# Moving the value sum's rounding and remainder behind the next score chunk's sigmoid in an attention kernel with two matrix layers

## The chip, the cores and the metric

The kernel runs on one core of a Trainium2 chip. The metric is the device time of one launch in microseconds (us). The engines that matter here are PE (TensorE: PE rows are matmuls, PEld rows are its weight loads), ACT (ScalarE), DVE (VectorE) and SP, whose only work is to issue transfers (DMAs) between the chip's main memory and on-chip memory. Every engine works through its own queue of instructions strictly in order. PSUM is the on-chip memory that matmuls write into.

## The reference

Batch 4, 12 heads, 448 positions, head width 64; then two layers with 768 model columns and 2048 hidden columns over 1792 tokens.

```
scores = scale * np.matmul(q, k.transpose(0, 1, 3, 2)) - np.log(S)
attn = 1.0 / (1.0 + np.exp(-scores))                 # sigmoid attention: no row sums
x = np.matmul(attn, v)                               # (B, H, S, D) -> (B * S, H * D)
h = x @ w_in1;  g = h - np.tanh(h);                  y = g @ w_out1
h = y @ w_in2;  r = np.maximum(h, 0.0);  g = s * (r * r) + b;  out = g @ w_out2
```

## The kernel before, in words

The work goes through the chip in two passes, each over two of the four batches: attention for twelve units, then layer 1, then layer 2. A **unit** is one batch and one pair of heads; units are numbered 0 to 23 over both passes, so that pass 1 has units 0 to 11 and pass 2 has units 12 to 23. The weights arrive as 8-byte words in pass 1; they are converted to float32 there (`w_conv`) and split into a rounded part and a remainder (`w_split`), and a float32 copy is written out for pass 2. The first three conversions and two splits lie between the attention units 5 to 9.

Most matmul operands are kept as a pair: a rounded upper part, made on ACT as a copy with a cast, and the remainder, made on DVE as the difference. The function `split` does that for the value sum.

The functions for one unit, all in program order on every engine (`keep_in_program_order`, line 80):

- `prep(i)` transposes q and k of unit i on PE into a PSUM tile `tqk`, lets ACT cast `qt` and `kt` from it, lets DVE make their remainders, and last lets DVE copy a piece to `qkf`, after which the tile is free.
- `qk(i, c)` makes the scores of one chunk of keys and applies the sigmoid on ACT (`af<-sc`). Chunk 3 has eight small matmuls from `qkf`; the chunks 0, 1 and 2 have six matmuls each from `qt` and `kt` and a sigmoid over 128x896.
- `av(i)` multiplies the sigmoid's tiles with the values (PSUM tiles `o` and `o2`). It is a generator: up to its `yield` stand the twenty matmuls of the trace; behind it ACT copies `o2` to `half`, DVE adds `half` to `o`, ACT casts `o` to `x` (the upper part), and DVE makes the remainder of `x`.

The main loop (lines 490 to 506) works on several units at once. One turn i issues the scores of chunks 0 and 1 of unit i, the conversion or split that is due, `prep(i + 1)`, the matmuls of `av(i - 1)`, chunk 3 of unit i, the rest of `av(i - 1)`, the loads of unit i + 3, and chunk 2 of unit i:

```
a = av(i - 1) if i > i0 else iter(())
next(a, None)
qk(i, 3)
now(a)
qkv_load(i + 3)
qk(i, 2)
```

On PE the scores of chunk 2 of unit i, and of chunks 0 and 1 of unit i + 1, stand directly behind each other, eighteen matmuls in all, and the transposes of unit i + 2 follow. The tiles `sc` and `tqk` share three PSUM buffers of two banks each (`banks`, tag "two"): a new tile has to wait until the reader of the tile that was in its buffer before is done. The transposes of `prep(i + 2)` go into the buffer that chunk 2 of unit i used. The tiles `o` and `o2` share two buffers of one bank each (tag "one").

q, k and v of a unit come in nine transfers of SP (`qkv_load`).

Of the kernel before, what the change touches and what calls it, by code (L numbers as in the profile page):

```python
# [19 lines left out]
def tile_kernel(ctx, tc, q, k, v, w_in1, w_out1, w_in2, w_out2, s_in, b_in, out):  # L20
# [63 lines left out]
    def banks(name):  # L84
        return ps_p.tile([P, 2, 512], F32, tag="two", name=name, bufs=3)
# [77 lines left out]
    def upto(step, n):  # L163

        while done[step] <= n:
            yield from step(done[step]) or ()
            done[step] += 1
# [10 lines left out]
    def now(g):  # L178
        for _ in g:
            pass  # L180
# [7 lines left out]
    def split(hi, lo, t):  # L188
        act.copy(hi, t)
        dve.tensor_tensor(out=lo, in0=t, in1=hi.bitcast(F32), op=ALU.subtract)  # L190
# [4 lines left out]
    def qkv_load(i, what="qkv"):  # L195
        if i >= B * NP:
            return
        b, hs = i // NP, slice(i % NP * 2, i % NP * 2 + 2)
        if "q" in what:
            raws[i] = {"r": at_p.tile([P, 2, D], F32, tag="rawr", name="rawr", bufs=3)}  # L200
        for nm in what:
            src = {"q": q, "k": k, "v": v}[nm]

            dma = act if i == 0 and nm == "k" else sp
            rest = src[b, hs, SM:S, :].rearrange("h p d -> p h d")
            if nm == "v":
                t = at_p.tile([P, 2, NJ + 1, D], F32, tag="rawv", name="rawv", bufs=4)

                tt, last = t[:, :, 0:NJ, :], t[0:RM, :, NJ, :]
                dma.dma_start(out=t[RM:P, :, NJ, :], in_=rest)  # L210
                dma.dma_start(out=tt.rearrange("p e j d -> p e (j d)"), in_=src[b, hs, 0:SM, :].rearrange("h (p j) d -> p h (j d)", p=P))
            else:
                t = at_p.tile([P, NJ, 2, D], F32, tag=f"raw{nm}", name=f"raw{nm}", bufs=3)

                o = RM * ((nm == "k") ^ (b % 2))
                last = raws[i]["r"][o:o + RM]
                for e in range(2):
                    dma.dma_start(out=t[:, :, e, :], in_=src[b, hs.start + e, 0:SM, :].rearrange("(p j) d -> p j d", p=P))
            dma.dma_start(out=last, in_=rest)
            raws[i][nm] = t  # L220

    def prep(i):

        if i >= B * NP:
            return
        b = i // NP
        rq, rk, rr = (raws[i][nm] for nm in "qkr")
        both = banks("tqk") if i else None


        if i:
            flat = both.rearrange("p a b -> p (a b)")
            parts = [(flat, 0), (flat, SM + P), (flat, SM)]
        else:

            one = [ps_p.tile([P, 512], F32, tag="one", name="tqk0", bufs=2) for _ in range(2)]
            parts = [(one[0], 0), (one[1], P), (one[0], SM), (one[1], 0)]
        for (ps, o), r in zip(parts, (rk, rq) if b % 2 else (rq, rk)):
            for j in range(NJ):
                pe.transpose(ps[:, o + j * P:o + (j + 1) * P], r[:, j].rearrange("p h d -> p (h d)"), ident)  # L240
        for ps, o in parts[2:]:
            pe.transpose(ps[:, o:o + P], rr.rearrange("p h d -> p (h d)"), ident)
        tq, tk = (flat[:, 0:S], flat[:, S:2 * S]) if i else (one[0][:, 0:S], one[1][:, RM:P + SM])
        if b % 2:
            tq, tk = tk, tq
        qt = at_p.tile([P, 2, S], F32R, tag="qt", name="qt", bufs=2)
        kt = at_p.tile([P, 2, S], F32R, tag="kt", name="kt", bufs=2)
        act.copy(qt[:, 0], tq)
        act.copy(kt[:, 0], tk)
        for t, ps in ((qt, tq), (kt, tk)):  # L250
            dve.tensor_tensor(out=t[:, 1], in0=ps, in1=t[:, 0].bitcast(F32), op=ALU.subtract)

        flt[i] = tmp_p.tile([P, WN], F32, tag="t2", name="qkf", bufs=2)
        dve.tensor_copy(flt[i], (flat if i else one[0])[:, SM:S + S] if b % 2 else (flat if i else one[0])[:, 0:S + RM])
        ready[i] = qt, kt
        avs[i] = []

    def qk(i, c):

        b = i // NP  # L260
        qt, kt = ready[i]
        sc = banks("sc")
        if c == NJ:

            f = flt.pop(i)
            kl, qf = (f[:, 0:RM], f[:, RM:]) if b % 2 else (f[:, S:], f[:, 0:S])
            for h in range(2):
                for e in range(2):
                    hs = slice(e * D, e * D + D)
                    pe.matmul(sc[h * RM:h * RM + RM, e, :SH], kl[hs], qf[hs, h * SH:h * SH + SH], start=True, stop=True)  # L270
            avs[i].append(g_p.tile([P, 2, 2, S], F32, tag="g", name="af", bufs=4))
            act.activation(avs[i][-1][:, 1, :, :SH], sc[:, :, :SH], AF.Sigmoid, bias=nlogs, scale=SCALE)
            return
        k0 = c * P if b % 2 else c * P + RM
        for n, (wi, xi) in enumerate(((0, 0), (0, 1), (1, 0))):
            for e in range(2):
                hs = slice(e * D, e * D + D)
                pe.matmul(sc[:, e, :S], kt[hs, wi, k0:k0 + P], qt[hs, xi], start=n == 0, stop=n == 2)
        if c == 0:
            avs[i].append(g_p.tile([P, 2, 2, S], F32, tag="g", name="af", bufs=4))  # L280
        act.activation(avs[i][-1][:, c % 2], sc[:, :, :S], AF.Sigmoid, bias=nlogs, scale=SCALE)

    def av(i):

        b, hp = i // NP, i % NP
        rv, af = raws.pop(i)["v"], avs.pop(i)
        o = ps_p.tile([P, 512], F32, tag="one", name="o", bufs=2)[:, :S]

        o2 = ps_p.tile([P, 512], F32, tag="one", name="o2", bufs=2)[:, :SH]
        for c in range(NJ):  # L290
            for e in range(2):
                pe.matmul(o[e * D:e * D + D], rv[:, e, c, :], af[c // 2][:, c % 2, e], start=c == 0, stop=False)
        for h in range(2):
            for e in range(2):
                ks = slice(h * RM, h * RM + RM)
                pe.matmul((o2 if h else o[:, :SH])[e * D:e * D + D], rv[ks, e, NJ, :], af[1][ks, 1, e, :SH], start=h == 1, stop=True)
        yield
        half = tmp_p.tile([P, WN], F32, tag="t1", name="half", bufs=2)[:, :SH]
        act.copy(half, o2)
        dve.tensor_tensor(out=o[:, SH:], in0=o[:, SH:], in1=half, op=ALU.add)  # L300
        if b % 2 == 0:
            x_t[b // 2, hp] = x_p.tile([P, 2, T2], F32R, tag="x", name="x1", bufs=CC)
        ns = slice(b % 2 * S, b % 2 * S + S)
        xt = x_t[b // 2, hp]
        split(xt[:, 0, ns], xt[:, 1, ns], o)
# [182 lines left out]
    for sb in range(B // 2):  # L488
        i0, i1 = sb * 2 * NP, (sb + 1) * 2 * NP
        for i in range(i0, i1):  # L490
            if i == 0 or i > i0:
                qk(i, 0)
                qk(i, 1)

            for at, step, n in ((2, w_load, 1), (4, w_load, 2), (5, w_conv, 0), (6, w_split, 0), (7, w_load, 3), (7, w_conv, 1), (8, w_split, 1), (9, w_load, 4), (9, w_conv, 2)):
                if i == at:
                    now(upto(step, n))
            if i + 1 < i1:
                prep(i + 1)
            a = av(i - 1) if i > i0 else iter(())  # L500
            next(a, None)
            qk(i, 3)
            now(a)
            qkv_load(i + 3)
            qk(i, 2)
            ready.pop(i)
        order = [(0, range(CC - 2)), lambda: now(av(i1 - 1)), (1, range(CC - 1)), (0, range(CC - 2, CC)), (1, [CC - 1])]

        turn[0] = 3
        x2 = layer1(sb, order)  # L510
        last = sb + 1 == B // 2
        order = [(0, range(CC - 1)), (1, range(CC - 1)), (0, [CC - 1]), (1, [CC - 1])]
        layer2(sb, x2, order, {} if last else {2: lambda: prep(i1), 4: lambda: qk(i1, 0), 6: lambda: qk(i1, 1)})
# [30 lines left out]
```

## Time and profile before

| | |
|---|---|
| median of three runs | 1125.86 us (1124.82 to 1127.56) |
| the profiled execution | 1124.64 us, of which the span is 1122.8 us |
| PE busy | 1098.6 us, 98% of the span |
| DVE, ACT busy | 585.5 us (52%), 493.7 us (44%) |
| granted TensorE clock | 1.0 |

The profiled execution is 1.22 us below the median of the runs and 1.84 us longer than its own span. The profile gives for each engine its instructions in order of time, how long the engine stood idle ahead of one and which event ended that wait. A share of busy time is a mean over the attention parts and the layers, which differ.

### The profile page before, as it was taken

The numbers are of one execution on the slowest core, as the hardware profiler recorded it, in microseconds if no ns is written. First come the engines' busy times: TensorE is split into PE (matmuls) and PEld (weight loads), VectorE is DVE, ScalarE is ACT, GpSimd is POOL, SyncE is SP. The second block draws the span as 40 slices with busy tenths as digits, with TensorE's granted clock in tenths as the row PEclk, the third lists the DMA queues.
The fourth block names the chain that finished last, engine by engine and source line by source line (L and its number), as shares of the span: only waits on it lengthen the run. The fifth ranks groups of instructions, "written<-read, shape, count | busy, mean of one in ns | idle before, by whom it ended". The sixth has DMA issues, their size and how long they took to land.

```text
span 1122.8 us, 15139 instructions
## 1 busy us (share of the span) xinstructions
PE 1098.6 (98%) x6077; PEld 949.4 (85%) x6077; DVE 585.5 (52%) x878; ACT 493.7 (44%) x782; POOL 0.7 (0%) x6
## 2 busy tenths in 40 slices
PE   8899999999999999999998899999999999999998
PEld 4446889888889999898964578898888899999998
DVE  3453656767787668686633332343434541434343
ACT  5775444242446563635356643332313363515060
POOL 0000000000000000000000000000000000000000
PEclk9999999999999999999999999999999999999999
DMA  4765454546455645454444301121211121211102
GB/s 112 201 152 148 156 185 154 169 146 192 127 169 168 203 136 183 133 189 130 167 113 113 79 29 57 48 66 43 71 43 46 54 71 43 60 53 57 57 15 99
DMA packets 115430, 124.47 MB, mean 111 GB/s; under 512 B 56480, under 2 KB 90784, under 8 KB 115360
## 3 DMA queue, kind: packets, MB, share of 16 engines
q1 hardware_dynamic: 114416, 123.27, 36.6%
q8 instruction: 48, 0.79, 0.3%
q10 hardware_dynamic: 944, 0.23, 0.1%
q14 instruction: 22, 0.18, 0.0%
HBM read 92.80 MB, written 30.67 MB: 110 GB/s over the span
## 4 chain that ended last, share of the span: by engine, by line
PE 92%; DMA 3%; DVE 2%; ACT 2%; SPq 1%; issue 1%; ACTq 0%; DVEq 0%
PE h L80 42%; PE z L80 21%; PE y L80 20%; PE o L80 6%; PE sc L80 2%; PE tqk L80 2%; SPq L80 1%; ACT af L80 1%; DMA rawq<-in_q_dram 1%; DMA rawv<-in_v_dram 1%; DMA rawk<-in_k_dram 1%; DMA win<-wf 1%; DVE wa L80 0%; DVE o L80 0%; DVE qt L80 0%
## 5 line engine op out<-in xcount | busy, mean ns | idle before, releaser
L80 PE MATMUL h<-x,whi 128*128 128x512 f32 (+1 forms) x1536 | 434.4, 363 | 0.0
L80 PEld LDWEIGHTS h<-x,whi 128*128 128x128 f32 x1536 | 283.4, 188 | 33.9 <-issue 1.3
L80 PE MATMUL h<-x,wlo 128*128 128x512 f32 (+1 forms) x768 | 279.8, 364 | 0.0
L80 PE MATMUL z<-whi,g 128*128 128x384 f32 x896 | 229.5, 334 | 0.0
L80 PE MATMUL y<-g,whi 128*128 128x512 f32 (+1 forms) x768 | 218.6, 366 | 0.2 <-DVE y L80 0.2
L80 ACT ACTIVATE t<-h 128x512 f32<-128x512 f32 (+1 forms) x128 | 69.6, 544 | 234.3 <-PE h L80 233.7
L80 PEld LDWEIGHTS z<-whi,g 128*128 128x128 f32 x896 | 162.0, 188 | 0.6 <-issue 0.6
L80 PEld LDWEIGHTS y<-g,whi 128*128 128x128 f32 x768 | 142.4, 188 | 17.7 <-DVE y L80 0.6
L80 PEld LDWEIGHTS h<-x,wlo 128*128 128x128 f32 x768 | 144.1, 188 | 15.2
L80 DVE TENSOR_TENSOR wlo<-wf,whi 128x768 fp32r<-128x768 f32 x128 | 122.0, 953 | 59.7 <-ACT whi L80 59.7
L80 ACT CAST whi<-wf 128x768 fp32r<-128x768 f32 x128 | 106.1, 833 | 101.9 <-DVE wf L80 58.0
L80 PE MATMUL z<-wlo,g 128*128 128x384 f32 x448 | 149.7, 334 | 0.0
L80 PE MATMUL y<-g,wlo 128*128 128x512 f32 (+1 forms) x384 | 140.9, 367 | 0.0
L80 DVE TENSOR_TENSOR g<-t,g 128x512 fp32r<-128x512 f32 (+1 forms) x128 | 79.9, 624 | 83.5 <-ACT g L80 83.5
L80 ACT ACTIVATE af<-sc,nlogs 128x896 f32<-128x896 f32 (+1 forms) x96 | 83.1, 919 | 48.4 <-PE sc L80 39.0
L80 ACT CAST g<-t 128x512 fp32r<-128x512 f32 (+1 forms) x128 | 72.7, 568 | 33.2 <-DVE t L80 30.9
L80 DVE TENSOR_TENSOR t<-h,t 128x512 f32<-128x512 f32 x64 | 39.9, 623 | 85.4 <-ACT t L80 85.4
L80 PEld LDWEIGHTS z<-wlo,g 128*128 128x128 f32 x448 | 84.1, 188 | 0.0
L80 PEld LDWEIGHTS y<-g,wlo 128*128 128x128 f32 x384 | 72.1, 188 | 8.9 <-DVE wlo L80 0.4
L80 DVE TENSOR_TENSOR z<-z 128x384 f32<-128x384 f32 x84 | 45.2, 554 | 65.8 <-PE z L80 65.8
L80 PE MATMUL o<-af,rawv 128*64 128x448 f32 (+1 forms) x480 | 72.4, 478 | 0.0
L80 DVE TENSOR_TENSOR y<-y 128x512 f32<-128x512 f32 x72 | 41.5, 618 | 58.0 <-PE y L80 58.0
(42 smaller groups left out, 674.9 us busy)
## 6 DMA issues: line engine op xcount, KB each, us to landing
raw<-in_moe_w_in_dram SPq DMA_DIRECT2D x32, 768.0 KB, 5.2
raw<-in_moe_w_out_dram SPq DMA_DIRECT2D x32, 768.0 KB, 4.8
win<-wf SPq DMA_DIRECT2D x32, 384.0 KB, 2.6
wout<-wf SPq DMA_DIRECT2D x32, 384.0 KB, 2.6
wf<-win SPq DMA_DIRECT2D x32, 384.0 KB, 3.0
wf<-wout SPq DMA_DIRECT2D x32, 384.0 KB, 3.0
rawq<-in_q_dram SPq DMA_DIRECT2D x48, 96.0 KB, 2.7
rawv<-in_v_dram SPq DMA_DIRECT2D x24, 192.0 KB, 2.7
```

The source lines that it names most:

```text
L80: return lambda *a, **kw: tc.keep_in_program_order(getattr(self.engine, name)(*a, **kw))
```

## The change

`av` gets a second `yield`, between DVE's sum with `half` and the split of `o` into `x`. The main loop takes the first part of what stood behind the old `yield` (the copy to `half` and the sum) where it stood, and runs the rest (the cast to `x` and its remainder) behind chunk 2 of the scores.

```
         half = tmp_p.tile([P, WN], F32, tag="t1", name="half", bufs=2)[:, :SH]
         act.copy(half, o2)
         dve.tensor_tensor(out=o[:, SH:], in0=o[:, SH:], in1=half, op=ALU.add)
+        yield
         if b % 2 == 0:
             x_t[b // 2, hp] = x_p.tile([P, 2, T2], F32R, tag="x", name="x1", bufs=CC)
...
             a = av(i - 1) if i > i0 else iter(())
             next(a, None)
             qk(i, 3)
-            now(a)
+            next(a, None)
             qkv_load(i + 3)
             qk(i, 2)
+            now(a)
             ready.pop(i)
```

On ACT this is the queue of turn 1 of pass 1, before (-) and now (+). `af<-sc` with 128x2x224 is the sigmoid of chunk 3; the three with 128x896 are the sigmoids of chunk 2 of this unit and chunks 0 and 1 of the next; `x_270` and `x_291` are the same tile under two names.

```order
 L80 ACTIVATE af<-sc,nlogs 128x2x224
 L80 COPY half<-o_249 128x224
-L80 CAST x_270<-o 128x448
-L80 ACTIVATE af<-sc,nlogs 128x896 x3
+L80 ACTIVATE af<-sc,nlogs 128x896
+L80 CAST x_291<-o 128x448
+L80 ACTIVATE af<-sc,nlogs 128x896 x2
 L80 CAST qt<-tqk 128x448
 L80 CAST kt<-tqk 128x448
```

The cast to `x` and the sigmoid of chunk 2 have changed places; nothing else on ACT has moved. The same stands in turns 1 to 11 and 13 to 23.

On DVE the queue of that turn is the same as before but for the numbers in the names; the rows are those of the changed kernel. `o<-o,half` is the sum, the row of `x_291` is the remainder of the cast.

```order
L80 TENSOR_TENSOR o<-o,half 128x224
L80 TENSOR_TENSOR x_291<-o,x_291 128x448
L80 TENSOR_TENSOR qt<-tqk,qt 128x448
L80 TENSOR_TENSOR kt<-tqk,kt 128x448
L80 COPY qkf<-tqk 128x512
```

The remainder still stands ahead of the next unit's `qt`, `kt` and `qkf`, though it now waits for a cast that stands one sigmoid later on ACT.

At the end of pass 1, in turn 11, ACT has no further sigmoids behind the cast; `o_1123` belongs to the last value sum, which stands within layer 1.

```order
 L80 ACTIVATE af<-sc,nlogs 128x2x224
 L80 COPY half<-o_1064 128x224
-L80 CAST x_601<-o 128x448
-L80 ACTIVATE af<-sc,nlogs 128x896
+L80 ACTIVATE af<-sc,nlogs 128x896
+L80 CAST x_622<-o 128x448
 L80 COPY half<-o_1123 128x224
```

Here too the two have changed places. The queues of PE and SP hold the same instructions in the same order as before.

## Rows read from the trace of the kernel before

**Rows 1.** Windows: span A:B, length, busy of each engine, granted clock, DMA share, GB/s

```profile
14.00:95.00 81.00, 71.48 (x576) 38.45 (x574) 36.91 (x63) 56.55 (x89) 0.00 (x0) 1.00 0.66 166
142.00:300.00 158.00, 158.00 (x779) 141.04 (x778) 111.12 (x157) 62.86 (x97) 0.00 (x0) 1.00 0.54 168
575.00:649.00 74.00, 65.67 (x555) 37.11 (x553) 27.77 (x50) 49.65 (x81) 0.00 (x0) 1.00 0.39 95
```

**Rows 2.** PE's waits, 14 to 95 us (pass 1): total, times, longest

```profile
PE tqk L80 <- ACT af L80: 6.0, 7, 0.9
PE tqk L80 <- DMA rawq<-in_q_dram: 1.7, 2, 1.2
PE tqk L80 <- DMA rawk<-in_k_dram: 1.1, 2, 0.7
```

**Rows 3.** PE's waits, 560 to 650 us (pass 2)

```profile
PE tqk L80 <- ACT af L80: 4.6, 5, 0.9
PE tqk L80 <- DMA rawv<-in_v_dram: 3.7, 4, 0.9
```

**Rows 4.** Timeline of one turn of pass 2: start, busy, engine, instruction [idle before]

```profile
594.43 2.81 ACT L80 ACTIVATE af<-sc,nlogs 128x896 f32<-128x896 f32 x3
...
595.50 0.55 PE L80 MATMUL tqk<-ident,rawq 128*128 128x128 f32 x3 [0.91 <-ACT af L80]
...
597.11 0.55 ACT L80 CAST qt<-tqk 128x448 fp32r<-128x448 f32 x1
...
597.52 0.57 ACT L80 CAST kt<-tqk 128x448 fp32r<-128x448 f32 x1
...
598.82 0.21 PEld L80 LDWEIGHTS o<-af,rawv 64*64 64x64 f32 x8 [0.70 <-issue]
...
599.20 0.68 DVE L80 COPY qkf<-tqk 128x512 f32<-128x512 f32 x1
...
599.74 2.09 PE L80 MATMUL sc<-qt,kt 64*128 64x448 f32 x18
599.93 0.64 ACT L80 ACTIVATE af<-sc,nlogs 128x448 f32<-128x448 f32 x1 [1.84 <-PE sc L80]
...
600.47 0.34 ACT L80 COPY half<-o 128x224 f32<-128x224 f32 x1
600.84 0.40 DVE L80 TENSOR_TENSOR o<-o,half 128x224 f32<-128x224 f32 x1 [0.95 <-ACT half L80]
601.27 0.53 ACT L80 CAST x<-o 128x448 fp32r<-128x448 f32 x1 [0.47 <-DVE o L80]
601.70 2.81 ACT L80 ACTIVATE af<-sc,nlogs 128x896 f32<-128x896 f32 x3
601.84 0.62 DVE L80 TENSOR_TENSOR x<-o,x 128x448 fp32r<-128x448 f32 x1 [0.60 <-ACT x L80]
...
602.76 0.55 PE L80 MATMUL tqk<-ident,rawk 128*128 128x128 f32 x3 [0.94 <-ACT af L80]
```

**Rows 5.** Timeline of turn 9 in pass 1, which converts a weight chunk

```profile
77.17 0.55 PE L80 MATMUL tqk<-ident,rawk 128*128 128x128 f32 x3 [0.52 <-DMA rawq<-in_q_dram]
...
81.40 2.89 PE L80 MATMUL sc<-qt,kt 64*128 64x448 f32 x18
...
82.68 0.68 DVE L80 COPY qkf<-tqk 128x512 f32<-128x512 f32 x1
...
85.19 0.55 PE L80 MATMUL tqk<-ident,rawk 128*128 128x128 f32 x3 [0.91 <-ACT af L80]
```

**Rows 6.** The chain that ended last, pass 1: start, length, what

```profile
35.23 4.29 DMA rawk<-in_k_dram
39.66 0.63 PE tqk L80 x4
```

**Rows 7.** k's transfers of unit 10: issue times, time from issue to landing

```profile
L80 SPq DMA_DIRECT2D rawk<-in_k_dram x2: 604/612/619, 70.3 to 71.0; - x2
...
DMA to landing us min/median/max: 4.2/4.4/4.6
```

**Rows 8.** SP's own waits, 14 to 100 us, the largest total

```profile
SPq L80 <- PE sc L80: 1.1, 3, 0.7
```

More of the change, by code (lines that the diff above doesn't have):

```diff
@@ L300, in av @@
         dve.tensor_tensor(out=o[:, SH:], in0=o[:, SH:], in1=half, op=ALU.add)
+        yield
         if b % 2 == 0:
@@ L502, in tile_kernel @@
             qk(i, 3)
-            now(a)
+            next(a, None)
             qkv_load(i + 3)
             qk(i, 2)
+            now(a)
             ready.pop(i)
```

## The prediction

> **What bounds the kernel now.** I read the windows first. In the layers PE has no idle time: 158.00 us busy of 158.00 [rows 1]. What the change does can therefore only be earned in the two attention stretches, where PE is busy 71.48 of 81.00 us and 65.67 of 74.00 us [rows 1]; and since PE is the bound right behind each stretch, what is earned there should stay earned to the end. Next I read what PE waits for. In pass 2 it is one gap, nine times, 4.6 + 3.7 = 8.3 us, always ahead of the transposes `tqk` [rows 3]. In pass 1 the same gap stands with 6.0 us in 7 waits, and beside it 1.7 + 1.1 us in 4 waits for q and k [rows 2].
>
> The timeline of one turn shows where the gap comes from [rows 4]. Let t be the start of the eighteen score matmuls, 599.74. ACT runs the sigmoid of chunk 3 at t + 0.19, the copy `half` at t + 0.73, then stands idle 0.47 us until DVE has made the sum, casts `x` at t + 1.53, and only at t + 1.96 starts the sigmoid of chunk 2, whose six matmuls are the first of the eighteen and long over. The transposes need the PSUM buffer that this sigmoid reads; they start 1.06 us after it, at t + 3.02, though the eighteen end at t + 2.09. That is the 0.94 us of the gap. One turn lasts 602.76 - 595.50 = 7.26 us.
>
> The four waits put down to `rawv` are the same gap: they have the same longest length, 0.9 [rows 3], and the transposes read q and k, not v. I count them as waits for the sigmoid.
>
> **The change, part by part.** It adds no instruction and no transfer. It takes the sum's round trip through DVE and the cast out of the way of chunk 2's sigmoid, and puts the cast, and with it the remainder, one sigmoid later.
>
> *The sigmoid of chunk 2.* It can start when `half` is off ACT and its six matmuls are done. A cast of 0.53 us lets the next instruction start 0.43 us after it (601.27 to 601.70), so `half` with 0.34 us should take about 0.24, which gives t + 0.97. Six of eighteen matmuls take a third of 2.09, t + 0.70, and somewhat more until the last one's result is there. I take t + 1.00. The transposes follow 1.06 us later, at t + 2.06, or when the eighteen are over, at t + 2.09. So they move from t + 3.02 to t + 2.09, which is 0.93 us per turn [rows 4]. Below, the gain could be nothing, if something else holds the transposes; above, it cannot exceed the gap, 0.94.
>
> *The next bound.* With a turn of 7.26 - 0.93 = 6.33 us, another ring has to be looked at: ACT and DVE must have freed the next unit's `tqk` buffer when chunk 0 wants it [rows 4]. From t: sigmoid of chunk 2 at + 1.00; the pitch of a large sigmoid is (597.11 - 594.43) / 3 = 0.89; so the cast starts at + 1.89, the two other sigmoids at + 2.32 and + 3.21, the cast `qt` at + 4.10, `kt` 0.41 later at + 4.51, `qkf` 599.20 - 597.52 = 1.68 after that at + 6.19, over at + 6.87. Chunk 0 wants the buffer about 0.70 into the next eighteen, and a wait takes 0.04 us to end where `x`'s remainder waits for its cast (601.80 to 601.84), which I round up to at most 0.2. So the next t cannot come before + 6.21 to + 6.37. It is as tight as PE's own path. I take 6.35 us for the turn, a gain of 0.91.
>
> *The remainder and what is queued behind it.* `x`'s cast moves from t + 1.53 to t + 1.89 and its remainder from 601.84 to about 602.2, over at 602.8. Behind it on DVE wait `qt`, `kt` and `qkf`, which need casts that come later still, at + 4.10; so it holds up nothing. PE waits for it as well, since `o2` of the next value sum takes the buffer it reads; that part of the value sum starts 598.82 - 595.50 = 3.32 us after the transposes, by the new times at about t + 5.4, against t + 3.1. In the turn that ends a pass the cast is some 0.4 us late, and `x` is first wanted in layer 1, several us behind. Cost nothing; cover 2 us or more.
>
> *Pass 2.* Nine gaps [rows 3], 0.91 each: 8.2 us. Ends: 0 and 8.3.
>
> *Pass 1* is different, because transfers stand beside the gap. SP issues without pause: its largest total of waits over 86 us is 1.1 us [rows 8]. So the q and k of a unit land when SP and the DMA engines get to them, and not earlier because PE is ahead. Two landings bind. k of unit 5 lands at 35.23 + 4.29 = 39.52, and its transposes start at 39.66 [rows 6]: everything gained up to there is lost again, as PE waits for this today. From there the gaps are regained, each about 0.9, some more in turns where a weight chunk is converted, until unit 10. The second of its two k transfers is issued at 71.0 and lands 4.6 later, at 75.6 [rows 7], where the transposes now start at 77.17 [rows 5]. Without the landing they would come 3 us earlier or more (four of the seven waits for the sigmoid, 0.86 each on the mean [rows 2], lie between 39.66 and these transposes); with it, 77.17 - 75.6 = 1.57 us. Turn 9, from there to 85.19, is 8.02 us long: it has a gap of 0.91, and its eighteen matmuls take 2.89 instead of 2.09, as chunk 1 waits there for `qkf`, over at 83.36, behind a weight conversion [rows 5]. The conversion doesn't wait for these transposes, so it runs ahead by what was gained before the landing, and `qkf` should be done by about 80.5, before chunk 1 wants it at 81.3. Of the 0.80 I leave 0.2 to be waited for (chunk 3's sigmoid ends at t + 0.83 [rows 4] and frees a buffer here too). That is 0.91 + 0.6 = 1.5. Pass 1: 1.57 + 1.5 = 3.1 us. Ends: 0, if SP sets the pace to the end, and 6.0 + 1.7 + 1.1 = 8.8, if no landing binds.
>
> What the row on SP shows, a queue that hardly waits [rows 8], has a rule in the Trainium skill, Perfetto Trace Analysis, section What "DMA-bound" means: a stretch is DMA-bound where the issuing engine's track is solid with transfers. By that rule alone pass 1 would give nothing and the sum would be 8.2; by the landings against PE's waits, 2.8 us for transfers and 6.0 for the sigmoid [rows 2], it gives 3.1.
>
> *Sum.* 8.2 + 3.1 = 11.3 us. The profiled execution took 1124.64, so 1113.3; it stood 1.22 below the median of the runs, 1125.86, which gives 1114.6. I say 1114.
>
> **The rivals.**
>
> *Pass 1 is held by its transfers to the end.* If k of unit 11 or q of unit 10 lands later than I read, or a faster PE meets the landings of every unit, only pass 2 gains: 8.2 us, 1116.4 to 1117.7. For it speaks that SP never rests; against it, that 7 of the 11 waits in pass 1 are for the sigmoid.
>
> *No landing binds in pass 1.* The rows of one execution give single landings; the two that bind took 4.29 and up to 4.6 us [rows 6, 7]. Were such ones 2 us quicker, pass 1 would give 6 to 8.8 and the time would be 1107 to 1111. Against it: the landing at 39.52 is on the chain that ended last [rows 6].
>
> *The gap stays and only changes its cause.* It is a wait for a PSUM buffer, and no buffer is added. If the ring through ACT and DVE, which I put at 6.35 us, is really 0.9 longer, because a few waits take 0.2 more than I read, chunk 0 waits for `qkf` in place of the transposes waiting for the sigmoid, and the turn stays at 7.26: 1124 to 1127. Against it: every link of the ring but one, the pitch of `half`, stands in a row. The Trainium skill, Perfetto Trace Analysis, section Optimization Strategy, says of a gap that repeats that it can mean too little SBUF or PSUM for the next tile; by that rule this change, which adds no buffer, leaves the gap. The trace agrees that a buffer is waited for, but shows its reader sitting ready on ACT for about 1 us, held by order alone.
>
> *Slower: the sigmoid becomes a cork.* Today the cast goes while chunk 2's matmuls run; now it, the remainder on DVE and all that is queued behind both wait until those matmuls are done. If PE reached chunk 2 late, the whole ring would slip by as much. From 0.91 us of delay beyond t + 1.00 it eats the gain, and each 0.3 us more costs 0.3 in some 20 turns, 6 us: 1131. Against it: on PE the six matmuls stand at the head of the eighteen, at t itself, and nothing in the rows holds them there.
>
> **How the numbers follow.** My forecast gets 0.63, the held pass 1 0.16, the free pass 1 0.08, the unchanged gap 0.08, the cork 0.05. Faster by more than 0.3% (3.4 us, about what a measurement of this kernel can tell from no change) holds in the first three: 0.87; same 0.08; slower 0.05. The range reaches from 1109, most of the way into the free pass 1, to 1119, which takes in the held pass 1 and a pass 2 that gives 0.2 us less per turn; outside are some 2 in 10.
>
> **What would show it.** In the changed profile the sigmoid of chunk 2 starts about 1.0 us after the eighteen and directly behind `half`; ACT's 0.47 us of idle time ahead of the cast is gone. PE's waits ahead of `tqk` in pass 2 fall from 8.3 us to under 1, and the turn from 7.26 to about 6.35, perhaps with small waits of chunk 0 for `qkf`. In pass 1 the waits for the sigmoid shrink while those for q and k grow, above all at units 5 and 10, the first at the same 39.66. Layer 1 starts about 3 us earlier in pass 1, about 11 in pass 2, and the layers' lengths stay. I would be wrong if the transposes in pass 2 still waited 0.5 us or more, or if PE waited in the layers for weights that now come too late.

## The result, and the profile after

The changed kernel takes 1115.53 us (median of 4 runs, 1113.83 to 1117.16), the kernel before in the same comparison 1125.34 (4 runs, 1124.77 to 1127.56). The ratio is 0.9909, with a 95% interval from 0.9888 to 0.993. The profiled execution took 1114.92 us, with a span of 1113.1; before it was 1124.64 and 1122.8, so the two executions differ by 9.7 us, where the sum of the prediction says 11.3.

The first matmul of layer 1 (`h<-x,whi`) marks the end of an attention stretch, so its two starts split the gain between the passes. In the timeline of PE before they read:

```profile
95.58 0.74 PE L80 MATMUL h<-x,whi 128*128 128x512 f32 x2
...
649.46 0.74 PE L80 MATMUL h<-x,whi 128*128 128x512 f32 x2
```

and after:

```profile
94.26 0.74 PE L80 MATMUL h<-x,whi 128*128 128x512 f32 x2
...
639.76 0.73 PE L80 MATMUL h<-x,whi 128*128 128x512 f32 x2
```

Up to the first mark 95.58 - 94.26 = 1.32 us are gained. Between the marks it is 649.46 - 95.58 = 553.88 against 639.76 - 94.26 = 545.50, which is 8.38 us. Together that is 9.70, the whole difference of the spans; the layers behind the second mark neither gain nor lose.

**Pass 2.** PE's waits from 565 to 645 us after the change are one row (engine, line, tile, releaser: total, times, longest), where [rows 3] has nine gaps with 8.3 us:

```profile
PE sc L80 <- ACT af L80: 0.3, 1, 0.3
```

One turn of pass 2 after, from its eighteen score matmuls to the next (start, busy, engine, instruction, idle before), beside [rows 4]:

```profile
589.30 2.17 PE L80 MATMUL sc<-qt,kt 64*128 64x448 f32 x18
589.49 0.63 ACT L80 ACTIVATE af<-sc,nlogs 128x448 f32<-128x448 f32 x1 [1.46 <-PE sc L80]
...
590.02 0.34 ACT L80 COPY half<-o 128x224 f32<-128x224 f32 x1
590.25 1.02 ACT L80 ACTIVATE af<-sc,nlogs 128x896 f32<-128x896 f32 x1
590.39 0.40 DVE L80 TENSOR_TENSOR o<-o,half 128x224 f32<-128x224 f32 x1 [0.57 <-ACT half L80]
591.15 0.54 ACT L80 CAST x<-o 128x448 fp32r<-128x448 f32 x1
...
591.40 0.55 PE L80 MATMUL tqk<-ident,rawq 128*128 128x128 f32 x3
...
591.73 0.62 DVE L80 TENSOR_TENSOR x<-o,x 128x448 fp32r<-128x448 f32 x1 [0.93 <-ACT x L80]
...
593.35 0.57 ACT L80 CAST qt<-tqk 128x448 fp32r<-128x448 f32 x1
...
595.46 0.68 DVE L80 COPY qkf<-tqk 128x512 f32<-128x512 f32 x1
...
595.63 0.67 PE L80 MATMUL sc<-qt,kt 64*128 64x448 f32 x4
```

With t = 589.30, chunk 2's sigmoid starts at t + 0.95, directly behind `half`; the cast follows at t + 1.85 with no idle time; the transposes start at t + 2.10, without a wait, as the eighteen end. The next eighteen come 595.63 - 589.30 = 6.33 us later. From the transposes at 578.75 to those at 629.31, eight turns later, a turn is 6.32 us on the mean, against 7.26 before.

**Pass 1.** PE's waits from 14 to 93 us, where [rows 2] has 6.0 us for the sigmoid and 2.8 for q and k:

```profile
PE tqk L80 <- DMA rawk<-in_k_dram: 3.7, 4, 1.5
PE tqk L80 <- DMA rawq<-in_q_dram: 0.6, 1, 0.6
PE sc L80 <- ACT half L80: 0.4, 2, 0.2
PE tqk L80 <- ACT x L80: 0.3, 1, 0.3
```

The waits for the sigmoid are gone here as well, but those for q and k have grown from 2.8 to 4.3 us. They have really grown by 2.0: of the 2.8 us, the 0.52 ahead of unit 10's transposes at 77.17 [rows 5] belong to the sigmoid, since that unit's q had landed at 74.12 and its k at 75.59. The chain that ended last (start, length, what) shows where the k of units 5 and 10 landed:

```profile
35.87 5.23 DMA rawk<-in_k_dram
...
41.23 0.63 PE tqk L80 x4
...
72.09 4.90 DMA rawk<-in_k_dram
76.98 0.14 issue
77.12 0.95 PE tqk L80 x7
```

In [rows 6] the first landing was at 39.52 and the transposes at 39.66; here they are at 41.23, later than before. In [rows 5] unit 10's transposes stood at 77.17, and here they stand at 77.12: all that was gained up to there is lost again.

Something else shows here that the kernel before had not shown. These are the windows of after (span A:B, length, busy of each engine, granted clock, DMA share, GB/s):

```profile
14.00:25.00 11.00, 8.52 (x67) 4.78 (x66) 3.13 (x6) 7.00 (x10) 0.00 (x0) 1.00 0.40 91
25.00:30.00 5.00, 5.00 (x31) 1.78 (x29) 1.75 (x3) 0.97 (x2) 0.00 (x0) 0.67 0.56 130
30.00:41.00 11.00, 9.14 (x82) 5.58 (x74) 3.80 (x7) 8.87 (x14) 0.00 (x0) 1.00 0.84 234
41.00:47.00 6.00, 5.77 (x34) 2.30 (x36) 1.75 (x3) 0.97 (x2) 0.00 (x0) 0.72 0.46 105
47.00:92.00 45.00, 43.99 (x346) 23.69 (x346) 26.05 (x43) 37.10 (x59) 0.00 (x0) 1.00 0.72 181
```

The granted TensorE clock has a mean of 0.67 and 0.72 in two of them, so it was at the lower of its two levels, 1.2 instead of 2.4 GHz, for a part of each. Both stretches begin with the end of a wait for k, in PE's timeline:

```profile
24.62 0.63 PE L80 MATMUL tqk<-ident,rawk 128*128 128x128 f32 x3 [1.47 <-DMA rawk<-in_k_dram]
...
25.40 4.44 PE L80 MATMUL o<-af,rawv 128*64 128x448 f32 x20
...
41.23 0.52 PE L80 MATMUL tqk<-ident,rawk 128*128 128x128 f32 x3 [1.45 <-DMA rawk<-in_k_dram]
```

The value sum behind the first wait takes 4.44 us; at the full clock it takes 3.02 (592.31 in the same trace).

### The profile page after: what moved, and what is told of

Read it like the earlier page. It is cut to its first block, busy times and chain, and to the rows that moved or that the text cites. A ratio compares the mean times of both kernels' runs of the same rounds, so it can differ in the third digit from the quotient of the medians.

```text
span 1113.1 us, 15139 instructions
## 1 busy us (share of the span) xinstructions
PE 1100.2 (99%) x6077; PEld 948.9 (85%) x6077; DVE 585.5 (53%) x878; ACT 491.9 (44%) x782; POOL 0.7 (0%) x6
## 2 busy tenths in 40 slices
DMA packets 115430, 124.47 MB, mean 112 GB/s; under 512 B 56480, under 2 KB 90784, under 8 KB 115360
## 4 chain that ended last, share of the span: by engine, by line
PE 94%; SPq 2%; DVE 1%; DMA 1%; ACT 1%; issue 0%; DVEq 0%; ACTq 0%
PE h L80 42%; PE z L80 21%; PE y L80 20%; PE o L80 6%; PE sc L80 4%; SPq L80 2%; PE tqk L80 1%; DMA rawk<-in_k_dram 1%; ACT af L80 0%; DVE wa L80 0%; DVE x L80 0%; DVE wf L80 0%; DVE y L80 0%; DVE wlo L80 0%; ACT x L80 0%
## 5 line engine op out<-in xcount | busy, mean ns | idle before, releaser
L80 ACT ACTIVATE af<-sc,nlogs 128x896 f32<-128x896 f32 (+1 forms) x96 | 86.1, 928 | 48.5 <-PE sc L80 39.1
L80 PE MATMUL o<-af,rawv 128*64 128x448 f32 (+1 forms) x480 | 75.5, 493 | 0.0
```

The source lines that it names most:

```text
L80: return lambda *a, **kw: tc.keep_in_program_order(getattr(self.engine, name)(*a, **kw))
```

## The experiments

The theory is that of the prediction: in pass 2 the order on ACT alone held PE; in pass 1 the gain is limited by when q and k land, and SP, which issues them, sets that. Its rivals: pass 1 gives nothing whatever the order; what matters is the place of the copy and the sum, not of the cast; what is lost in pass 1 is lost to something other than SP. The first four kernels ran on one chip against 1125.08 (15 runs of the kernel before), the next four against 1125.53 (7), the last two against 1124.74 (11). Each edit is against the changed kernel.

**pass2_only** has the new order in pass 2 alone.

```
-            next(a, None)
+            if sb == 1:
+                next(a, None)
+            else:
+                now(a)
             qkv_load(i + 3)
```

> The new order in pass 2 alone. Theory (in pass 2 the gap was pure order, in pass 1 the landing of unit 10's k takes most of it back): 8.3 us less than before, 1117, PE's waits ahead of the transposes in pass 2 near 0, pass 1 as before. Rival (both passes gain alike, the profiled execution of the changed kernel was unlucky in pass 1): also 8.3, so this run alone fixes the share of pass 2; what is left to the changed kernel's 9.8 is pass 1.

Measured: 1117.44 us, ratio 0.9926 (0.9913 to 0.9938). From the first `h` at 97.02 to that of pass 2 at 642.52 it is 545.50 us, as in the changed kernel: pass 2 gives 8.38 by itself. Pass 1, in the old order, ended 1.44 us later here than in the profile before. Its waits ahead of `tqk` are 8.9 us in all, as before (8.8 [rows 2]); but one value sum, at 25.59, took 4.52 us in place of 3.02, at a mean clock of 0.72 from 25 to 31 us. So pass 1 varies between executions of the same instructions.

**pass1_only** has it in pass 1 alone: the same edit with `sb == 0`.

> The new order in pass 1 alone. Theory (transfers hold pass 1): 1 to 2 us less than before, about 1124, with waits for k ahead of the transposes of units 3, 5 and 10 in place of those for the sigmoid. Rival (my sum): 3.1 us less, 1122.

Measured: 1122.77 us (11 runs, 1121.61 to 1126.03), ratio 0.998 (0.9971 to 0.9989): 2.3 us, between the theory's 1 to 2 and the rival's 3.1. The profiled execution, 1121.61 us, is the quickest of the 11, and it shows the prediction's own picture; four rows of PE's timeline:

```profile
38.33 0.52 PE L80 MATMUL tqk<-ident,rawq 128*128 128x128 f32 x3 [1.97 <-DMA rawq<-in_q_dram]
39.16 0.52 PE L80 MATMUL tqk<-ident,rawk 128*128 128x128 f32 x3 [0.30 <-DMA rawk<-in_k_dram]
...
75.62 0.52 PE L80 MATMUL tqk<-ident,rawk 128*128 128x128 f32 x3 [1.79 <-DMA rawk<-in_k_dram]
...
92.51 0.74 PE L80 MATMUL h<-x,whi 128*128 128x512 f32 x2
```

Unit 10 starts at 75.62, where 75.6 was forecast, and `h` at 92.51, 3.07 us ahead of before. The difference to the changed kernel's profile, whose code in pass 1 is the same, lies in SP's queue: there the two k transfers of unit 10 were issued from 71.44 on and had landed at 76.98, here they were issued from 69.44 on and had landed at 75.48 (before: 70.31 and 75.59). So pass 1 gives 3.1 us where the transfers come in good time, and less where not.

**all_behind** moves the copy `half` and the sum behind chunk 2's sigmoid as well.

```
             qk(i, 3)
-            next(a, None)
             qkv_load(i + 3)
             qk(i, 2)
             now(a)
```

> The copy to half and DVE's sum go behind chunk 2's sigmoid too, in both passes. Theory (the ring through ACT and DVE is as tight as PE's own path): the sum's round trip of some 0.5 us idle on ACT comes back into the ring, behind the sigmoid, so the turn in pass 2 is 6.7 to 6.9 us instead of 6.32, PE waits for qkf ahead of chunk 0 and not ahead of the transposes, and the kernel is 3.5 to 5 us slower than the changed one, 1119 to 1120. Rival (only chunk 2's sigmoid counts, it may go as early as it likes): the same as the changed kernel within 1 us, 1115 to 1116.

Measured: 1118.78 us, ratio 0.9944 (0.9931 to 0.9956), 3.25 us above the changed kernel's 1115.53 (the theory says 3.5 to 5). PE's waits in pass 2, 565 to 645 us:

```profile
PE sc L80 <- DVE qkf L80: 3.1, 5, 0.6
PE sc L80 <- ACT af L80: 0.3, 1, 0.3
```

In every second turn PE stops within the eighteen matmuls, behind the six of chunk 2:

```profile
582.80 0.87 PE L80 MATMUL sc<-qt,kt 64*128 64x448 f32 x6
584.30 1.50 PE L80 MATMUL sc<-qt,kt 64*128 64x448 f32 x12 [0.63 <-DVE qkf L80]
```

The waits ahead of the transposes are gone here too, but chunk 0 now waits for `qkf`, as the theory has it; turns alternate between 7.17 and 6.27 us ((632.25 - 578.56) / 8 = 6.71 on the mean). With 0.34 us of copy and the sum's round trip moved ahead of the cast, `qkf` starts 589.73 - 582.80 = 6.93 us after the eighteen began; in the changed kernel it is 595.46 - 589.30 = 6.16. The ring through ACT and DVE is as tight as the prediction puts it, and where the copy stands does matter.

**w_spread** issues the first three weight loads in turns 1, 3 and 5, not two in turn 2 and one in turn 4, where they stand ahead of q and k of unit 5.

```
-((2, w_load, 1), (4, w_load, 2), (5, w_conv, 0),
+((1, w_load, 0), (3, w_load, 1), (5, w_load, 2), (5, w_conv, 0),
```

> The changed kernel, with the first three weight loads issued in turns 1, 3 and 5 of pass 1 instead of two in turn 2 and one in turn 4, so that no two of 768 KB stand ahead of unit 5's q and k. Theory (landings hold pass 1, unit 5's k because of the weights ahead of it): the wait ahead of unit 5's transposes falls from 2.1 us to under 1, but unit 10, behind the load of turn 7, still binds, so the whole gains 0 to 1 us over the changed kernel, 1115. Rival (SP's pace of issue alone holds pass 1): unit 5 waits as long as before and nothing changes at all.

Measured: 1114.58 us, ratio 0.9907 (0.9891 to 0.9922). Unit 5 no longer waits: its k is issued at 33.22 and the first of its two transfers has landed at 35.77, 2.6 us later, where in after it took from 35.11 to 39.62, 4.5 us. Units 2, 4, 6, 8 and 10 wait instead:

```profile
PE tqk L80 <- DMA rawk<-in_k_dram: 6.4, 5, 2.0
```

But for unit 2 these are the units whose loads are the first behind a weight load. So the rival, SP's pace alone, falls: a weight load costs SP one issue like any other, but what stands behind it lands late. The sum hardly moves, since the wait moves to other units.

**after_again** is the changed kernel once more, as a measure for the runs beside it.

> The changed kernel once more, unchanged. Theory (transfers hold pass 1, and they land at other times in every execution, so that the gain of pass 1 swings between about 1 and 3 us): the layers of pass 1 start 1 to 3 us before the 95.58 us of the kernel before, with waits for q and k at other units than in the first profile; pass 2 again 8.4 us shorter. Rival (the first profile shows what the change does in pass 1): the same waits at units 3, 5 and 10, layers from 94.3.

Measured: 1114.27 us (1114.0 to 1115.53), ratio 0.9904 (0.9889 to 0.9918). `h` starts at 93.34 and 638.84: pass 1 gives 2.24 us, pass 2 again 8.38. The waits sit at units 2, 5 and 10, and none at unit 3. One of them, 1.32 us ahead of unit 5's transposes, is put down to the sigmoid in the profile, but that had ended at 37.73 and the unit's q landed at 39.06, just ahead of the transposes at 39.19.

**one_dma** loads q of a unit in one transfer for both heads, and so k: seven issues of SP for each unit in place of nine, and the same bytes (124.46 and 124.47 MB in all, in 114662 and 115430 packets).

```
-                for e in range(2):
-                    dma.dma_start(out=t[:, :, e, :], in_=src[b, hs.start + e, 0:SM, :].rearrange("(p j) d -> p j d", p=P))
+                dma.dma_start(out=t, in_=src[b, hs, 0:SM, :].rearrange("h (p j) d -> p j h d", p=P))
```

> The changed kernel with one transfer for both heads of q, and one for k, in place of two each: SP issues 7 transfers for a unit instead of 9, with the same bytes and the same packets. Theory (SP's pace of issue sets when q and k land): 1.2 us less issue per unit, the waits ahead of the transposes in pass 1 go but for the odd one, the layers of pass 1 start 2 to 4 us earlier than in the changed kernel, 1111.5 to 1113.5. Rival (the DMA engines set it, busy with the weights): SP is earlier, transfers take longer to land, and the time stays at 1115.

Measured: 1106.23 us (1105.91 to 1106.47), ratio 0.983 (0.9815 to 0.9844). PE's waits from 10 to 94 us, all of attention in pass 1:

```profile
PE tqk L80 <- DMA rawq<-in_q_dram: 0.9, 1, 0.9
PE sc L80 <- ACT af L80: 0.5, 1, 0.5
PE sc L80 <- ACT half L80: 0.5, 2, 0.2
PE tqk L80 <- DMA rawk<-in_k_dram: 0.2, 1, 0.2
```

SP's issues for a unit's q and k heads (and one pair more of k), first in the changed kernel, then here:

```profile
40.45 1.27 SPq L80 DMA_DIRECT2D rawq<-in_q_dram  x2
...
42.43 1.27 SPq L80 DMA_DIRECT2D rawk<-in_k_dram  x2
...
56.81 2.40 SPq L80 DMA_DIRECT2D rawk<-in_k_dram  x2
```

```profile
39.23 0.62 SPq L80 DMA_DIRECT2D rawq<-in_q_dram  x1
...
40.61 0.62 SPq L80 DMA_DIRECT2D rawk<-in_k_dram  x1
```

In the rows of the one unit an issue takes SP about 0.62 us, for 96 KB as for 192 KB; others in attention of pass 1 take longer, as the row at 56.81 shows, up to 1.75 us in the changed kernel and 2.26 here. Two fewer in each unit give back 1.3 us of a queue that a unit keeps for 6.61 us (40.45 to 47.06 in the changed kernel, with one weight load), while PE wants a unit every 6.3. From 14 to 80 us the DMA engines moved 194 GB/s here and 160 in after, so in after they were not at their limit over that stretch. `h` starts at 85.28, 8.06 us ahead of after_again, and pass 2 stays at 545.47. This was more than I had expected: the first units gain as well, since nine issues each stand ahead of them too.

**v_pool** leaves q and k alone and lets POOL issue the three v transfers of the units 3 to 11.

```
-            dma = act if i == 0 and nm == "k" else sp
+            dma = act if i == 0 and nm == "k" else pool if nm == "v" and 2 < i < NP * 2 else sp
```

> The changed kernel with v's three transfers of the units 3 to 11 issued by POOL, which is idle there. Theory (SP's pace): SP has 6 issues per unit left, 2 us less; waits for q and k in pass 1 go, 2 to 4 us less than the changed kernel, if POOL's transfers land in time for the value sums. Rival (DMA engines): 1115, or slower if POOL's issue is slow and the value sums wait for v.

Measured: 1110.21 us, ratio 0.9866 (0.9851 to 0.988). Waits for k are left at units 2 and 3 alone (1.9 us), whose loads stand ahead of POOL's share. The same bytes over the same DMA engines, issued from two queues, come in time. This edit changes more than SP's load, though: POOL's transfers go through a queue of their own, 2.36 MB in 1152 packets, so that v no longer stands ahead of the next unit's q and k, and the packets fall from 115430 to 111542 in all.

**fill** asks what the fallen clock costs: two matmuls of zeros go into `tqk` ahead of the transposes of units 3, 5 and 10, and are overwritten by them.

```
+            if i in (3, 5, 10):
+                for n in range(2):
+                    pe.matmul(both[:, n, :S], zero[:, :P], zero, start=True, stop=True)
```

> The changed kernel with two more matmuls of zeros ahead of the transposes of units 3, 5 and 10, into the tile that the transposes fill afterwards, so that PE works while it would wait for k. Theory (the fall of the granted clock behind such a wait is an effect of the wait and costs little, since the next landing binds anyway): granted clock 1.0 and value sums of 3.0 us in place of 4.4 and 4.7, time within 1 us of the changed kernel. Rival (the fallen clock is what took 1.8 us of my sum): 1113 to 1114.

Measured: 1113.67 us (1113.06 to 1114.19), ratio 0.9895 (0.9878 to 0.9911), 0.6 below after_again, whose runs overlap with it; the number fits the theory and the rival alike. The clock did not fall behind units 3 and 5; it fell behind a wait of 1.72 us at unit 2, which has no fill. That decides nothing on the cost.

**before_one_dma** is the kernel before, in its old order, with the loads of one_dma; beside that edit it takes the change back.

```
-        yield
...
-            next(a, None)
+            now(a)
...
-            now(a)
```

> The kernel before, in the old order, with one transfer for both heads of q and one for k. Theory (transfers hid most of what the new order is worth in pass 1; without them the old order has its gap of 0.5 to 0.9 us at all nine or ten units there): the early start and the waits for transfers are gained, about 4 to 5 us, 1120.5 to 1121.5, and the new order is then worth 14 to 15 us in all (against 1106.2), 6 to 7 of them in pass 1. Rival (the two edits add up): 9.3 us less than before, 1116 to 1117, and the new order worth 10 on it as on the kernel before.

Measured: 1121.02 us (1120.56 to 1122.26), ratio 0.9965 (0.9951 to 0.9979). PE's waits from 10 to 94 us:

```profile
PE tqk L80 <- ACT af L80: 7.5, 9, 0.9
PE sc L80 <- ACT af L80: 0.5, 1, 0.5
PE sc L80 <- DVE qkf L80: 0.3, 2, 0.2
```

With transfers out of the way pass 1 has the same nine gaps as pass 2, and 0.8 us of other waits. Against this kernel the new order (one_dma) is worth 1121.02 - 1106.23 = 14.8 us; by the marks 91.81 - 85.28 = 6.5 in pass 1 and 553.89 - 545.47 = 8.4 in pass 2. The fewer issues give the old order 3.7 us and the new one some 8 (1114.27 - 1106.23): each hides a part of what the other is worth.

**one_dma_spread** joins one_dma and w_spread.

> The changed kernel with one transfer for both heads and with the first three weight loads in turns 1, 3 and 5. Theory (only unit 5 still waits, 1.1 us, behind two weight loads): up to 1 us less than with one transfer alone, 1105.2. Rival (a weight load alone delays the q and k behind it as much): other units wait instead, 1106 to 1107.

Measured: 1105.69 us (1105.52 to 1106.81), ratio 0.9829 (0.9813 to 0.9844). It is the quickest version, 9.8 us below the changed kernel and 19 below the kernel before, but not to be told from one_dma: q and k of one unit are still waited for, 0.5 and 0.2 us. It is now unit 4, again the first behind a weight load; in one_dma it was unit 5.

## Why the prediction was right, and where a size was off

**The sigmoid of chunk 2.** Right in each link: it starts at t + 0.95 (forecast 1.00), 0.23 us after `half` (0.24, worked out from a longer cast), the cast at t + 1.85 (1.89), the transposes at t + 2.10 (2.09) [rows 4].

**The next bound.** A turn is 6.32 us, for 6.35. Only the 0.2 us that I had allowed for the end of waits were too much. That this ring is really next, all_behind shows: a little more work ahead of `qkf`, and chunk 0 waits 0.6 us in every second turn.

**The remainder.** Cost nothing, as said; it starts at 591.73, and `qkf` at 595.46 is in time.

**Pass 2.** 8.38 us for 8.2 in after, after_again and pass2_only, and 8.42 in one_dma against before_one_dma. The mechanism and the size are shown. The rival by which the gap stays under another name fell with it. With it fell, for this case, the reading that the prediction took from the Trainium skill, Perfetto Trace Analysis, section Optimization Strategy, that a gap that repeats can mean too little PSUM for the next tile: here it went with no buffer added.

**Pass 1** is the term that was mis-sized: 3.1 us forecast, 1.32 in the profile after, 2.24 in after_again, 3.07 in that of pass1_only. The mechanism holds: the waits for the sigmoid go, those for q and k grow, and units 5 and 10 bind. Of the two parts of the sum, the 1.5 us of turn 9 came as forecast or nearly so; the 1.57 us ahead of unit 10's transposes, which rest on its k landing at 75.6, did not:

| profile | k of unit 10 has landed | its transposes, gain | turn 9, gain |
|---|---|---|---|
| before | 75.59 | 77.17 | 8.02 |
| after | 76.98 | 77.12, 0.05 | 6.73, 1.29 |
| after_again | 76.29 | 76.42, 0.75 | 6.51, 1.51 |
| pass1_only | 75.48 | 75.62, 1.55 | 6.51, 1.51 |

The step that failed is thus the one that takes the landings of one execution as fixed, "lands 4.6 later, at 75.6"; unit 5's "its transposes start at 39.66" was not fixed either (41.23 in after), but what is lost there goes into the same term, as unit 10 waits for its k in all three. The landing came up to 1.4 us later than forecast, and took the gain with it. The rival that pass 1 is held by its transfers was half true in the profiled execution of after.

What makes q and k late lies in SP's queue, and there in two things. One is its pace: in one_dma, with two issues fewer per unit and the same bytes, the waits all but go, and units 2 and 3, which have no weight load ahead of them, waited too in after (0.54 and 1.47 us). The other is the weight loads in the same queue: the second k transfer of units 5 and 10, behind such loads, took 5.23 and 4.90 us to land in after, against a median of 2.8 for all of k's, and w_spread moved the waits with the loads. How the 8 us between after_again and one_dma divide between the two is not shown. The rule on the solid issue track in the Trainium skill, Perfetto Trace Analysis, section What "DMA-bound" means, names a limit that is really there once the sigmoid no longer holds PE. By it alone pass 1 would have given nothing, and it gave 1.32 to 3.07 us; in the old order, fewer issues were worth 3.7 us.

That the prediction's 1114 came nearer to the runs than its two terms to the profile is partly chance: pass 2 gave 0.2 us more and pass 1 0.9 to 1.8 less in the profiles of the changed kernel.

**The clock** was no step of the prediction. In pass2_only a stretch at the low clock went with unit 4's transposes coming 2.26 us later than in before (33.45 against 31.19), and `h` came 1.44 later. In after the value sums behind the two waits took 1.42 and 1.69 us more (4.44 and 4.71 at 41.79, less 3.02), but unit 10 still waited 0.22 us for its k, until 77.12: with the landing where it was, a quicker PE would have started there no earlier. That the landing would have come earlier with a quicker PE is not shown, and the idle time of SP gives no sign of it: between the 98 issues ahead of unit 10's k it is 5.5 to 5.6 us in the profiles of before, after, after_again and pass1_only alike. What drifts is the length of the issues themselves, 64.08, 65.11, 64.58 and 63.13 us in sum; about a dozen in each profile take more than 0.7 us. Why these take longer, and not always the same, is open. fill did not settle what the clock costs.

## What to carry to other kernels

Where an in-order engine holds a buffer's reader behind a round trip to another engine, let the reader go first and fill the round trip with it; and compare the ring through the other engines with the new pitch before adding one more thing to what is moved. Ask next which queue paces the transfers: a gain from compute is kept only where loads keep up, and the time that an execution's landings give is a sample, to be given a width. Two changes that relieve two limits in the same stretch can be worth more together than alone: here 19 us, against 10 for the order and 4 for the fewer issues.

## What the runs showed of the hardware that was not expected

The granted TensorE clock fell in attention of pass 1 in some executions and not in others, and the length of the wait ahead of it does not tell which. In after it fell behind waits of 1.47 and 1.45 us, in pass2_only behind one of 0.81; in after_again its mean was 0.50 from 16 to 22 us, behind a wait of 1.59, and the value sum there took 5.46 us. In pass1_only it stayed at 1.00 behind waits of 1.97 and 1.79 us, and in after_again the waits of 1.01 and 1.59 us at units 5 and 10 were followed by value sums of 3.02. In one_dma, with waits of at most 0.9 us, all value sums of pass 1 took 3.01 or 3.02 us.

The issue of a transfer took SP 0.62 us with 96 KB and with 192 KB in the rows shown, and up to 1.75 us elsewhere in attention of pass 1 of the changed kernel. Joining two transfers into one, over the same bytes, was worth 8 us of 1114.
